# Moving the logs, powers and phases of two groups to other places in the instruction order of a fused GateLoop attention and gated layer

## The chip, the cores and the metric

The kernel runs on one core of a Trainium2 chip. The metric is the device time of one execution in microseconds. Several runs of a kernel are told by their median. A separate, profiled execution gives the trace from which the lines below come.

## The reference

```python
mag = np.sqrt(a_re * a_re + a_im * a_im)
scale = np.minimum(mag, 0.999) / (mag + 1e-06)
a_re_n, a_im_n = (a_re * scale, a_im * scale)
for t in range(S):
    ar, ai = (a_re_n[:, :, t, :, None], a_im_n[:, :, t, :, None])
    new_re = ar * S_re - ai * S_im
    new_im = ar * S_im + ai * S_re
    kv = np.einsum('bhd,bhe->bhde', k[:, :, t], v[:, :, t])
    S_re, S_im = (new_re + kv, new_im)
    y[:, :, t] = np.einsum('bhd,bhde->bhe', q[:, :, t], S_re)
x = y.transpose(0, 2, 1, 3).reshape(3072, 384)
h = x @ w_in                     # w_in 384 x 2048
out = (h * np.cos(h)) @ w_out    # w_out 2048 x 384
```

There are 4 batches, 8 heads, 768 steps and a head size of 48. The activations are 32-bit floats. The two weight matrices arrive as 64-bit floats.

## The kernel before

**Tiling.** The 3072 rows are cut into 24 chunks of 128 steps. Two chunks make a group, so there are twelve groups, numbered from 0. This text calls group 0 the first, group 1 the second and group 2 the third. Within a chunk the recurrence is turned into a masked product of keys and queries that carry cumulative decay and phase. A state of 96 x 48 a head passes from chunk to chunk.

**Steps of a group.** `log_steps` (line 731) squares `re` and `im` on ScalarE, and computes from them the log of the decay (`lg`) and the tangent of the half angle (`tan`), on ScalarE and VectorE in turn. Its last operation, the check, reads `re` once more and sums what is below zero; for group 0 it writes to `below`, for the others over `re` itself. `p_powers` (line 790) sums the logs along the steps on TensorE (`lgs`) and takes two exponentials (`P`, `Q`). `g_angle` (line 836) is the arctangent. `g_phase` (line 855) sums the angles on TensorE (`phs`), a chunk at a time, and subtracts the whole turns: a cast on ScalarE, then a subtraction on VectorE. For the second chunk of group 1 the sum takes in the reduced phase of the first. `p_even`, `p_apply`, `g_trig` and `g_stack` make from these the keys `ks` and the queries `qs`, 128 x 16 x 96 each. For groups 0 and 1 TensorE turns them (`f_turn`, `tp`), and ScalarE copies them to `kT` and `qT`. From group 2 on `f_transpose` (line 894) does it: VectorE transposes blocks of 32 x 32 (`tr`), and SP's queue writes them to DRAM (`moved`) and reads them back in order as `kT` and `qT`.

**Attention and layer.** `f_scores` multiplies keys and queries (`sc`) and masks them on VectorE (`atm`). `f_state` (`sp`) carries the state, `f_out` (`yp`) gives the rows, and `f_xt` (line 1003) takes them through DRAM (`x`, `xT`). `mm1` (line 1015) makes one of the eight tiles of h for a group (`hp`, 128 x 512 in one PSUM bank, six products); then ScalarE takes its sine with a shift of a quarter turn (`gate`) and, as a bound check, its square (`junk`), and VectorE multiplies gate and h. The tiles go in turn to three banks: two with the tag `m`, one with the tag `acc`. A fourth tile so waits for the gate of the first. `mm2` (line 1034) multiplies the gates with `w_out` (`op`), 16 products for a chunk. This holds for groups 0 and 1; later groups use a scheme with seven smaller products (`seventh`).

**Weights.** `weight` (line 596) fetches 1/8 of a matrix at a time as raw 64-bit words through GpSimd's queue into four buffers (`raw`). Each part takes a step on ScalarE and three on VectorE (`as_floats`, line 621). `into` lists the eight parts of `w_in`, `back` those of `w_out`. The first four of `w_in` are fetched at the start.

**Order.** Each engine runs its instructions in one order, which the build fixes. The activations that need a table (`special`) and all matrix products are chained in program order. The other operations go where the build's scheduler puts them. Between lines 1227 and 1255 the order of VectorE and ScalarE is written out by hand (`Ordered.by_hand`). After that `weave` (line 1140) merges lists of steps: each list gets a stretch between 0 and 1, and its steps are spread evenly in it. ScalarE's table for logs and exponentials is not the one for sine and arctangent; a change of table is a load (`ACT_TABLE_LOAD`). `load` (line 550) puts loads on SP's queue, and `logs(g)` (line 1176) ends with the load of the next group's `re` and `im`.

Of the kernel before, what the change touches and what calls it, by code (L numbers as in the profile page):

```python
# [11 lines left out]
F32 = mybir.dt.float32  # L12
# [475 lines left out]
def fast_path(ctx, tc, q, k, v, a_re, a_im, moe_w_in, moe_w_out, out, least, odd, wide):  # L488
# [9 lines left out]
    C = 128  # L498
    NCH = S // C
    G = 2  # L500
# [19 lines left out]
    stage = {"pool": room.enter_context(tc.tile_pool(name="stage", bufs=1)), "bufs": 4}  # L520
# [22 lines left out]
    X = [dict() for _ in range(NG)]  # L543
# [6 lines left out]
    def load(g, names, i=None, put=nc.sync.dma_start):  # L550
        for name in names:
            ap = {"re": a_re, "im": a_im, "q": q, "k": k, "v": v}[name]
            if name not in X[g]:
                X[g][name] = ld.tile([C, G, H, D], F32, tag=name, name=name,
                                     bufs=2 if name == "v" else 1)
            b, c = divmod(g * G + (i or 0), NCH)
            one, n = i or 0, G if i is None else 1
            steps = ap[b].rearrange("h (c p) d -> p c h d", p=C)[:, ds(c, n)]
            tile_ = X[g][name][:, ds(one, n)]
            parts = [(0, C, 0)]  # L560
            if name in ("re", "im") and g >= PEG:
# [10 lines left out]
        for i in range(G):  # L572
            load(0, names, i)
    ident = constant(np.eye(C, dtype=np.float32), "ident", pool=stage["pool"])
    sums = [constant(sums_np[0], "sums", pool=stage["pool"])]
    turns = [constant(sums_np[0] * np.float32(1.0 / math.pi), "turns", pool=stage["pool"])]
    last = constant(last_np, "last", pool=stage["pool"])
    carry = constant(carry_np, "carry")
# [200 lines left out]
    def summed_up(ps, g, i, name, ones):  # L779

        if g < PEG:
            matmul(ps, lhsT=ones, rhs=cut(X[g][name], i, 1), start=True, stop=True)
            return
        chunks_ = range(i + 1) if name == "tan" else [i]
        terms = [(half, c) for half in ("hi", "lo") for c in chunks_]
        for half, c in terms:
            matmul(ps, lhsT=exact if c == i else alls, rhs=cut(X[g][half], c, 1),
                   start=((half, c) == terms[0]), stop=((half, c) == terms[-1]))

    def p_powers(g, i):  # L790

        x = X[g]
        if i == 0:
            x["P"], x["Q"] = x["lg"], temp("Q")
            x["row"] = rows_d.tile([G * DM], F32, tag="row", name="row")
            x["end"] = ft.tile([D2, G * H], F32, tag="end", name="end")
        ps = pa.tile([C, DM], F32, tag="a", name="lgs")
        summed_up(ps, g, i, "lg", sums[0])
        special(out=cut(x["P"], i, 1), in_=ps, func=AF.Exp)
        special(out=cut(x["Q"], i, 1), in_=ps, func=AF.Exp, scale=-1.0)  # L800

# [34 lines left out]
    def g_angle(g, i, n):  # L836

        at = cut(X[g]["tan"], i, n)
        special(out=at, in_=at, func=AF.Arctan)
# [15 lines left out]
    def g_phase(g, i):  # L855

        x, n = X[g], g * G + i
        ps = pa.tile([C, DM], F32, tag="a", name="phs")
        early = g < PEG and n % NCH
        if not early:  # L860
            summed_up(ps, g, i, "tan", turns[0])
        else:
            matmul(ps, lhsT=turns[0], rhs=cut(x["tan"], i, 1), start=True, stop=False)
            matmul(ps, lhsT=last, rhs=before(n), start=False, stop=True)
        ph = cut(x["tan"], i, 1)
        scalar.copy(out=ph.bitcast(I32), in_=ps)
        vector.tensor_tensor(out=ph, in0=ps, in1=ph.bitcast(I32), op=ALU.subtract)
# [144 lines left out]
            out=xt.rearrange("p c g t -> p c (g t)"),  # L1012
            in_=moved.rearrange("p s d t -> (p s d) t").rearrange("(c r) t -> r c t", r=C))

    def mm1(g, jp):
        x = X[g]
        third = len(x.setdefault("gate", {})) % 3 == 2
        ps = pm.tile([C, 2, G * C], F32, tag="acc" if third else "m", name="hp",
                     bufs=1 if third else 2)
        for ji in range(2):  # L1020
            for dc in range(ND):
                matmul(ps[:, ji], lhsT=w_in[:, jp, dc, ts(ji, C)],
                       rhs=x["xT"][:, dc].rearrange("p g t -> p (g t)"),
                       start=(dc == 0), stop=(dc == ND - 1))
        gate = msb.tile([C, 2, G * C], F32, tag="gate", name="gate", bufs=8)
        junk = msb.tile([C, 2, G * C], BF16, tag="junk", name="junk", bufs=1)
        special(out=gate, in_=ps, func=AF.Sin, scale=1.0 / in_scale, bias=half_pi_b)
        scalar.activation(out=junk, in_=ps, func=AF.Square, scale=1.0 / in_scale,
                          accum_out=wide[:, ds(g * (NJ // 2) + jp, 1)])
        gated = vector.tensor_tensor(out=gate, in0=ps, in1=gate, op=ALU.mult)  # L1030
        x.setdefault("gated", gated)
        x["gate"][jp] = gate

    def mm2(g, i, j0, nj):
        if j0 == 0:
# [128 lines left out]
    def turned(g, i, name):  # L1164
        return [lambda hh=hh: f_turn(g, i, name, hh) for hh in range(2)]

    def prods(g):
        if not 0 <= g < NG:
            return
        for i in range(G):  # L1170
            yield lambda i=i: p_powers(g, i)
        yield lambda: g_angle(g, 0, G)
        yield lambda: g_carry(g)
        yield lambda: (p_even(g, 0, G), p_apply(g, 0, G))

# [63 lines left out]
    for i in range(2):  # L1239
        p_even(0, i, 1)  # L1240
    g_phase(0, 0)
    g_phase(0, 1)
    g_trig(0, 0, 1)
    p_apply(0, 0, 1)
# [6 lines left out]
    for t in (turned(0, 0, "kT") + turned(0, 0, "qT") + early[:1]  # L1251
              + [lambda: f_scores(0, 0), lambda: f_scores(0, 1)] + early[1:2]
              + turned(0, 1, "kT") + turned(0, 1, "qT") + early[2:3]
              + [lambda: p_end(0, 0, 2), lambda: f_state(0), lambda: f_rows(0)]
              + [lambda: f_scores(1, 0), lambda: f_scores(1, 1), lambda: f_columns(0)]
              + [lambda: f_state(1), lambda: busy(4), lambda: f_rows(1)] + early[3:4]
              + [lambda: busy(2), lambda: f_columns(1), lambda: busy(2)]
              + [lambda: next(one, None), lambda: next(two, None),
                             lambda: load(2, ("v",))]):
        t()  # L1260
    weave((logs(1), 0.0, 0.1), (convert(into[RAW:]), 0.0, 0.5),
          (first(0), 0.2, 1.0), (prods(1), 0.55, 0.58), ([lambda: load(2, ("k", "q"))], 0.58, 0.6),
          (phases(1), 0.7, 0.8), (keys(1), 0.8, 0.9), (convert(back[:4]), 0.5, 1.0))
    over = [t for i in range(G) for name in ("kT", "qT") for t in turned(1, i, name)]
    weave((convert(back[4:]), 0.0, 0.3), (second(0, 0), 0.0, 0.65), (over, 0.2, 0.6),
          (logs(2), 0.3, 0.31), (chunks(1), 0.7, 1.0), (prods(2), 0.85, 0.87))
    room.close()
    stage.update(pool=ctx.enter_context(tc.tile_pool(name="late", bufs=1)), bufs=1)
    weave((second(0, 1), 0.0, 0.35), (phases(2), 0.2, 0.3), (keys(2), 0.3, 0.45),
          (first(1), 0.4, 1.0))  # L1270
    for n in range(2, NG):
        weave((mixes(n - 1, 2, 4), 0.0, 0.12), (logs(n + 1), 0.0, 0.02), (chunks(n), 0.0, 0.36),
              (second(n - 1, 0), 0.0, 0.38), (products(n - 1, 0, 3), 0.0, 0.36),
# [82 lines left out]
```

## Time and profile before

| what | value |
|---|---|
| median of 3 runs | 675.01 us (674.88 to 675.69) |
| profiled execution | 674.87 us |
| its span | 673.0 us |
| mean granted TensorE clock | 0.986 |
| TensorE busy | 649.9 us |
| VectorE busy | 490.5 us |
| ScalarE busy | 396.5 us |
| ACT_TABLE_LOAD | 26 times, 33.4 us |
| first product of `hp` | at 45.08 us |
| first score of the second group | at 95.29 us |
| last product of `phs` of the third group | ends at 115.2 us |
| first score of the third group | at 139.07 us |

Times in the trace are microseconds from the start of the span. A row of a timeline gives start, length, engine, line, operation, what is written and what is read, a count, and in brackets how long the engine was idle before, and who released it. Many rows name the lines of helpers: 686 is every matrix product, 675 every VectorE or ScalarE operation that needs no table, 706 every activation that needs one. The tile's name tells the steps apart. [...] a product can stand as two records.

### The profile page before, as it was taken

How to read it: one execution, taken by the hardware profiler on the slowest of the kernel's cores; microseconds unless marked ns; L12 is line 12 of the kernel's file. 1: busy time of each engine (PE TensorE's matmuls, PEld its weight loads, DVE VectorE, ACT ScalarE, POOL GpSimd, SP SyncE). 2: the span in 40 equal slices, each digit the busy share in tenths (PEclk: the TensorE clock that was granted, in tenths of full speed). 3: DMA queues.
4: the chain of work that ended last, by engine and by line, in shares of the span. 5: the costliest groups of instructions: out<-in, count | busy, mean ns of one | idle time of the engine just before them, and what ended most of it. 6: DMA issues, size and time to landing. Idle time of an engine off the chain costs nothing.

```text
span 673.0 us, 10725 instructions
## 1 busy us (share of the span) xinstructions
PE 649.9 (97%) x4055; PEld 579.6 (86%) x4055; DVE 490.5 (73%) x793; ACT 396.5 (59%) x730; POOL 27.8 (4%) x47
## 2 busy tenths in 40 slices
PE   7897899999999999999999999999999999999995
PEld 5685677886899889999899999999999999999895
DVE  4989987668867867877768778868778768862241
ACT  6779875483574575476477467467467467332330
POOL 2012000000000000000000000000000000000000
PEclk8989989999999999999999999999999999999998
DMA  9788725814824845955945864864864862363000
GB/s 252 162 244 234 188 67 116 215 41 87 220 58 92 214 119 122 230 119 118 234 119 118 216 136 117 214 138 116 218 141 116 215 140 87 115 143 105 24 6 24
DMA packets 232810, 94.90 MB, mean 141 GB/s; under 512 B 208798, under 2 KB 221217, under 8 KB 232748
## 3 DMA queue, kind: packets, MB, share of 16 engines
q1 hardware_dynamic: 226252, 68.62, 45.2%
q0 software_dynamic: 5632, 25.17, 11.4%
q8 instruction: 34, 0.56, 0.3%
q10 hardware_dynamic: 864, 0.33, 0.2%
q14 instruction: 28, 0.23, 0.1%
HBM read 69.28 MB, written 24.81 MB: 140 GB/s over the span
## 4 chain that ended last, share of the span: by engine, by line
PE 80%; ACT 6%; DVE 6%; DMA 6%; issue 2%; SPq 0%; ACTq 0%; DVEq 0%
PE hp L686 32%; PE op L686 17%; PE sum L686 14%; PE yp L686 6%; PE sc L686 5%; PE sp L686 3%; PE phs L686 2%; DMA re<-in_a_re_dram 1%; PE lgs L686 1%; ACT raw L675 1%; DMA qT<-moved 1%; DMA raw<-in_moe_w_in_dram 1%; DVE mag L675 1%; DMA raw<-in_moe_w_out_dram 1%; DVE tan L675 1%
## 5 line engine op out<-in xcount | busy, mean ns | idle before, releaser
L686 PE MATMUL hp<-xT,w_in 128*128 128x256 f32 x1152 | 253.1, 381 | 1.3 <-DVE gate L675 0.9
L686 PEld LDWEIGHTS hp<-xT,w_in 128*128 128x128 f32 x1152 | 219.9, 191 | 33.3 <-DVE gate L675 1.8
L706 ACT ACTIVATE gate<-hp,half_pi_b 128x512 f32<-128x512 f32 x96 | 65.9, 687 | 127.6 <-PE hp L686 127.6
L686 PE MATMUL op<-w_out,gate 128*128 128x192 f32 (+1 forms) x448 | 103.7, 377 | 3.1 <-DVE w_out L675 3.1
L675 DVE TENSOR_TENSOR gate<-hp,gate 128x512 f32<-128x512 f32 x96 | 65.7, 685 | 55.8 <-ACT junk L675 55.8
L686 PEld LDWEIGHTS op<-w_out,gate 128*128 128x128 f32 x448 | 75.9, 191 | 19.7 <-DVE w_out L675 4.1
L675 ACT ACTIVATE junk<-hp 128x512 bf16<-128x512 f32 x96 | 56.5, 589 | 0.0
L686 PE MATMUL sum<-t_s,s 128*128 128x192 f32 x320 | 55.4, 327 | 0.0
L686 PEld LDWEIGHTS sum<-t_s,s 128*128 128x128 f32 x320 | 52.5, 191 | 0.3 <-DVE ot L675 0.3
L675 DVE TENSOR_TENSOR atm<-sc,causal 128x512 f32<-128x512 f32 x48 | 32.8, 687 | 24.8 <-PE sc L686 24.8
L686 PE MATMUL sc<-qT,kT 96*128 96x128 f32 x384 | 49.3, 276 | 1.4 <-ACT qT L675 0.8
L686 PEld LDWEIGHTS sc<-qT,kT 96*128 96x128 f32 x384 | 47.8, 192 | 3.2 <-ACT qT L675 1.1
L675 ACT ACTIVATE ot<-sum 128x192 f32<-128x192 f32 x30 | 9.5, 319 | 49.8 <-PE sum L686 49.8
L702 ACT ACT_TABLE_LOAD x26 | 33.4, 1283 | 4.0 <-DMA ident<-ident_const 3.6
L675 DVE SCALAR_TENSOR_TENSOR ot<-op,ot 128x192 f32<-128x192 f32 x31 | 11.0, 355 | 32.5 <-ACT ot L675 23.9
L675 ACT CAST tan<-phs 128x384 int32<-128x384 f32 x24 | 11.5, 478 | 39.2 <-PE phs L686 39.2
L686 PE MATMUL yp<-atm,v 128*48 128x128 f32 x352 | 33.6, 277 | 0.0
L686 PEld LDWEIGHTS sp<-v,ks 128*96 128x96 f32 x320 | 29.7, 165 | 0.0
L686 PE MATMUL yp<-qT,state 96*48 96x128 f32 x304 | 29.7, 272 | 0.0
L686 PE MATMUL sp<-v,ks 128*96 128x48 f32 x320 | 29.6, 246 | 0.0
L686 PE MATMUL sum<-w_out,gate 128*128 128x192 f32 x160 | 29.6, 329 | 0.0
L686 PE MATMUL op<-t_a,gate 128*128 128x192 f32 x160 | 29.0, 333 | 0.0
(138 smaller groups left out, 997.2 us busy)
## 6 DMA issues: line engine op xcount, KB each, us to landing
moved<-tr SPq DMA_DIRECT2D x20, 768.0 KB
raw<-in_moe_w_in_dram POOLq DMA_DIRECT2D x16, 768.0 KB, 5.8
raw<-in_moe_w_out_dram POOLq DMA_DIRECT2D x16, 768.0 KB, 4.7
kT<-moved SPq DMA_DIRECT2D x40, 192.0 KB
qT<-moved SPq DMA_DIRECT2D x10, 768.0 KB
k<-in_k_dram SPq DMA_DIRECT2D x24, 192.0 KB
q<-in_q_dram SPq DMA_DIRECT2D x24, 192.0 KB
v<-in_v_dram SPq DMA_DIRECT2D x24, 192.0 KB
```

The costliest lines, as they stand in the source:

```text
L675: ins = getattr(self.engine, op)(**kw)
L686: chain(nc.tensor.matmul(out, **kw), "tensor")
L702: chain(nc.scalar.preload_act_table_set(table))
L706: chain(nc.scalar.activation(func=func, **kw))
```

## The change

The rest of the diff renames `sums` to `upto`.

```diff
-    def mm1(g, jp):
-        x = X[g]
-        third = len(x.setdefault("gate", {})) % 3 == 2
-        ps = pm.tile([C, 2, G * C], F32, tag="acc" if third else "m", name="hp",
-                     bufs=1 if third else 2)
+    def mm1_sums(g, jp):
+        x = X[g]
+        x.setdefault("gate", {})
+        order = x.setdefault("order", [])
+        home = "mmcamcmm"[jp] if g == 0 else "mmc"[len(order) % 3]
+        order.append(jp)
+        pool, tag, bufs = {"m": (pm, "m", 2), "c": (pm, "acc", 1), "a": (pa, "a", None)}[home]
+        ps = pool.tile([C, 2, G * C], F32, tag=tag, name="hp", **({"bufs": bufs} if bufs else {}))
...
+        x.setdefault("hp", {})[jp] = ps
+
+    def mm1_gate(g, jp):
+        x = X[g]
+        ps = x["hp"].pop(jp)
...
+    def mm1(g, jp):
+        mm1_sums(g, jp)
+        mm1_gate(g, jp)
...
+    def powers(g):
+        return [lambda i=i: p_powers(g, i) for i in range(G)]
+
     def prods(g):
         if not 0 <= g < NG:
             return
-        for i in range(G):
-            yield lambda i=i: p_powers(g, i)
-        yield lambda: g_angle(g, 0, G)
+        if g not in (1, 2):
+            yield from powers(g)
+            yield lambda: g_angle(g, 0, G)
         yield lambda: g_carry(g)
         yield lambda: (p_even(g, 0, G), p_apply(g, 0, G))
...
     g_phase(0, 0)
+    next(one, None), next(two, None)
     g_phase(0, 1)
...
-              + [lambda: next(one, None), lambda: next(two, None),
-                             lambda: load(2, ("v",))]):
+              + [lambda: load(2, ("v",))]):
         t()
-    weave((logs(1), 0.0, 0.1), (convert(into[RAW:]), 0.0, 0.5),
-          (first(0), 0.2, 1.0), (prods(1), 0.55, 0.58), ([lambda: load(2, ("k", "q"))], 0.58, 0.6),
-          (phases(1), 0.7, 0.8), (keys(1), 0.8, 0.9), (convert(back[:4]), 0.5, 1.0))
+    later = convert(into[RAW:])
+    for t in (list(logs(1)) + later[:1] + sums(0, 0, 3) + powers(1) + later[1:2] + sums(0, 3, 4)
+              + [lambda: g_angle(1, 0, G)] + gates(0, 0, 2) + phases(1) + gates(0, 2, 4)
+              + later[2:]):
+        t()
+    weave((first(0)[4:], 0.0, 1.0), (prods(1), 0.1, 0.2),
+          ([lambda: load(2, ("k", "q"))], 0.3, 0.32),
+          (keys(1), 0.35, 0.5), (convert(back[:2]), 0.7, 1.0))
     over = [t for i in range(G) for name in ("kT", "qT") for t in turned(1, i, name)]
-    weave((convert(back[4:]), 0.0, 0.3), (second(0, 0), 0.0, 0.65), (over, 0.2, 0.6),
-          (logs(2), 0.3, 0.31), (chunks(1), 0.7, 1.0), (prods(2), 0.85, 0.87))
+    weave((convert(back[2:]), 0.0, 0.4), (second(0, 0), 0.05, 0.65), (over, 0.1, 0.6),
+          (chunks(1), 0.7, 1.0))
     room.close()
     stage.update(pool=ctx.enter_context(tc.tile_pool(name="late", bufs=1)), bufs=1)
-    weave((second(0, 1), 0.0, 0.35), (phases(2), 0.2, 0.3), (keys(2), 0.3, 0.45),
-          (first(1), 0.4, 1.0))
+    for t in (list(logs(2)) + second(0, 1) + sums(1, 0, 2) + powers(2) + sums(1, 2, 3)
+              + [lambda: g_angle(2, 0, G)] + gates(1, 0, 3)):
+        t()
+    weave((first(1)[3:], 0.0, 1.0), (prods(2), 0.0, 0.02), (phases(2), 0.1, 0.3),
+          (keys(2), 0.35, 0.6))
```

`mm1` is split: `mm1_sums` is its products, `mm1_gate` its gate, square and multiplication. `sums` and `gates` list these for a range of tiles. The fourth `hp` tile of group 0 takes a bank of the pool `pa`, which the attention uses.

No operation is added or dropped but loads of ScalarE's table: the path that runs has 24 in place of 26. What moves on TensorE's queue, as the two builds have it (products of a kind in brackets):

```
before, group 1: hp(24) lgs hp(6) phs hp(6) phs hp(12), then op(16) with tp among them, scores
after,  group 1: hp(18) lgs hp(6) phs phs hp(24), then op(16) with tp among them, scores
before, group 2: scores of group 1 with lgs among them, op(12) phs op(4) hp(48), scores
after,  group 2: scores of group 1, op(16) hp(12) lgs hp(12) phs hp(24), scores
```

On ScalarE the check of group 0 stands between the casts of its two phases instead of behind copies of `kT` and `qT`; the powers of group 1 stand ahead of all gates of group 0; the powers and the arctangent of group 2 stand behind the last `ot` copy and ahead of the gates of group 1; the sines of group 2 stand behind the gate of the fifth `hp` tile. On VectorE the first part of `w_out` ends behind the last gate of group 0 and the keys of group 1; before, it ended ahead of the fifth gate. On SP's queue the load of `re` for group 1 stands ahead of four small loads of `end`, and the load of `v` for group 3 ahead of `xT` of group 1.

More of the change, by code (lines that the diff above doesn't have):

```diff
@@ L574, in fast_path @@
     ident = constant(np.eye(C, dtype=np.float32), "ident", pool=stage["pool"])
-    sums = [constant(sums_np[0], "sums", pool=stage["pool"])]
+    upto = [constant(sums_np[0], "sums", pool=stage["pool"])]
     turns = [constant(sums_np[0] * np.float32(1.0 / math.pi), "turns", pool=stage["pool"])]
@@ L797, in p_powers @@
         ps = pa.tile([C, DM], F32, tag="a", name="lgs")
-        summed_up(ps, g, i, "lg", sums[0])
+        summed_up(ps, g, i, "lg", upto[0])
         special(out=cut(x["P"], i, 1), in_=ps, func=AF.Exp)
@@ L1257, in fast_path, with sums, gates @@
               + [lambda: busy(2), lambda: f_columns(1), lambda: busy(2)]
-              + [lambda: next(one, None), lambda: next(two, None),
-                             lambda: load(2, ("v",))]):
-        t()
-    weave((logs(1), 0.0, 0.1), (convert(into[RAW:]), 0.0, 0.5),
-          (first(0), 0.2, 1.0), (prods(1), 0.55, 0.58), ([lambda: load(2, ("k", "q"))], 0.58, 0.6),
-          (phases(1), 0.7, 0.8), (keys(1), 0.8, 0.9), (convert(back[:4]), 0.5, 1.0))
+              + [lambda: load(2, ("v",))]):
+        t()
+    def sums(g, lo, hi):
+        return [lambda jp=jp: mm1_sums(g, jp) for jp in range(lo, hi)]
+    def gates(g, lo, hi):
+        return [lambda jp=jp: mm1_gate(g, jp) for jp in range(lo, hi)]
+    later = convert(into[RAW:])
[6 more added lines that the diff above has]
+          (keys(1), 0.35, 0.5), (convert(back[:2]), 0.7, 1.0))
     over = [t for i in range(G) for name in ("kT", "qT") for t in turned(1, i, name)]
-    weave((convert(back[4:]), 0.0, 0.3), (second(0, 0), 0.0, 0.65), (over, 0.2, 0.6),
-          (logs(2), 0.3, 0.31), (chunks(1), 0.7, 1.0), (prods(2), 0.85, 0.87))
+    weave((convert(back[2:]), 0.0, 0.4), (second(0, 0), 0.05, 0.65), (over, 0.1, 0.6),
+          (chunks(1), 0.7, 1.0))
     room.close()
     stage.update(pool=ctx.enter_context(tc.tile_pool(name="late", bufs=1)), bufs=1)
-    weave((second(0, 1), 0.0, 0.35), (phases(2), 0.2, 0.3), (keys(2), 0.3, 0.45),
-          (first(1), 0.4, 1.0))
+    for t in (list(logs(2)) + second(0, 1) + sums(1, 0, 2) + powers(2) + sums(1, 2, 3)
[3 more added lines that the diff above has]
+          (keys(2), 0.35, 0.6))
     for n in range(2, NG):
```

## The prediction

> **What bounds the kernel now.** I read the page's busy shares first, then TensorE's waits, then the stages, then the hand-over into the third group. The span is 673.0 us and the execution took 674.87 us, 0.14 us below the median of 675.01.
>
> ```profile
> PE 649.9 (97%) x4055; PEld 579.6 (86%) x4055; DVE 490.5 (73%) x793; ACT 396.5 (59%) x730; POOL 27.8 (4%) x47
> ```
>
> TensorE bounds it: 23.1 us idle in all. From the timeline, 6.9 us of that lie before 28 us and 7.2 us in the last stretch, from 600 us on; neither is touched. TensorE's waits (total, times, longest) name what is left:
>
> ```profile
> PE op L686 <- DVE w_out L675: 3.1, 1, 3.1
> PE phs L686 <- ACT tan L706: 3.1, 2, 2.9
> ...
> PE hp L686 <- DVE gate L675: 0.9, 2, 0.7
> ```
>
> Three of these, 0.73 + 2.88 + 3.14 = 6.75 us, lie between 54 and 84 us. That is what the change can take away. The stages show who sets that region (after the colon: length, busy PE, PEld, DVE, ACT, POOL, granted clock, DMA):
>
> ```profile
> 54.00:58.00 4.00, 3.27 (x15) 2.78 (x15) 4.00 (x8) 4.00 (x9) 0.52 (x1) 1.00 1.12 317
> 58.00:64.00 6.00, 3.50 (x15) 2.48 (x13) 6.00 (x9) 5.94 (x11) 1.44 (x2) 1.00 0.86 224
> 64.00:68.00 4.00, 3.62 (x8) 2.27 (x9) 4.00 (x6) 2.99 (x7) 0.72 (x1) 0.57 0.61 184
> ...
> 80.00:84.00 4.00, 0.86 (x4) 0.20 (x2) 4.00 (x9) 3.08 (x5) 0.00 (x0) 1.00 0.43 173
> ```
>
> VectorE is full in each, so moving its work about frees nothing by itself; and the clock is 0.57 just after a wait of 2.9 us. Then TensorE's timeline (start, length) around the third group:
>
> ```profile
> 115.00 0.34 PE L686 MATMUL phs<-lo,exact 128*128 128x384 f32 x1
> 115.18 2.74 PE L686 MATMUL op<-w_out,gate 128*128 128x384 f32 x8
> 117.76 8.04 PE L686 MATMUL hp<-xT,w_in 128*128 128x256 f32 x36
> 126.01 13.22 PE L686 MATMUL hp<-xT,w_in 128*128 128x256 f32 x60 [0.22 <-DVE gate L675]
> 139.07 1.06 PE L686 MATMUL sc<-qT,kT 96*128 96x128 f32 x8
> ```
>
> Between the last phase product and the first score lie 23.9 us of TensorE work. Under it runs the way from phases to turned queries. On SP's queue:
>
> ```profile
> 123.19 2.54 SPq L906 DMA_DIRECT2D moved<-tr  x2
> 127.14 3.89 SPq L909 DMA_DIRECT2D kT<-moved  x4
> 131.14 1.06 SPq L911 DMA_DIRECT2D qT<-moved  x1
> ```
>
> The stage 132 to 136 us has a DMA share of 1.00, 136 to 140 one of 0.10: qT lands near 136.4, 2.7 us ahead of its use. So cast, sines, products, two transposes and transfers take 136.4 - 115.2 = 21.2 us, all but 2.7 of 23.9 us.
>
> **What the Trainium skill says.** "TensorE: Matmul & The Clock Gate", What's actually happening: an idle TensorE falls to half clock and recovers after about 3.4 us of work. The trace agrees: the first phase product after the 2.88 us wait took 1.44 us, warm ones 0.65; together with what follows the two long waits cost 1.5 and 1.7 us more. The same page, Part 2: What happens when you issue a matmul, keeps matmuls in program order; "Perfetto Trace Analysis", Tensor Engine Instruction (MATMUL, LD_WEIGHTS), calls ScalarE and VectorE strict queues: a late operand stops all behind it. The trace agrees: the second group's logarithm, its input ready by 42.1 us, stood until 44.84 behind copies of which the first waited for TensorE until 43.03. "ScalarE: Activation LUTs", What ACT_TABLE_LOAD costs: 1283 ns and a drain of about 1380; here 1.28 us and the next operation starts at once (59.24 to 60.53), so I price 1.28.
>
> **The change, part by part.** Starts below that are not in the trace are my estimates, walked along the built queues with the trace's durations: VectorE start to start 0.87 us at 768 wide, 0.47 at 384 or for a one-input operation, 0.60 for a gate; on ScalarE a gate and its square 1.15, a weight part 0.9, four powers 1.5.
>
> *First check.* Its two operations (0.5 us each) move from 29.9 and 32.3 us into a ScalarE gap of 1.59 us (19.69 to 21.28): free. The second group's `re`, whose buffer they release, goes out near 24.3 us rather than 33.0, on SP's queue now ahead of four tiny `end` loads that VectorE needs at 36.3. The squares come near 30 us, not 39.5. Yet the logarithm stands on ScalarE behind the xT copy (44.47) in both queues: 44.84 as before. The squares stand ahead of four copies that TensorE needs at 34.5 and that ended at 32.4: room for 1.8 us if `re` is late. Value 0; bounds a gain of 0.6, a loss of 0.8.
>
> *Second group.* Two table loads (2.6 us of ScalarE) go away, and the 0.73 us wait. hp tiles 0 to 2 fill three banks until 54.0, sums of logs to 55.3, hp 3 to 58.0 in a bank of the other pool. ScalarE, done with logs at 51.4, idles until 54.8 for the sums, then powers 56.3, table 57.6, arctangent 58.4: the phase product waits 0.45 instead of 2.88. But the second half's phase needs the reduced first one, whose cast stands behind two gates (58.4 + 2.3 = 60.7, plus subtraction, behind a gate and a conversion step: 62.2); TensorE waits 1.8. hp 4 to 7 then run 62.9 to 73.3. VectorE after 62.2: gates 2 and 3 (64.0), even powers and phase (67.1), bit mask and k product (68.4), gate 4 behind three weight parts on ScalarE (69.2), then q product, gates 5 to 7 and the four key products (76.9). Only there does the first w_out part end, near 77.8; before, at 65.8. TensorE waits for it from 73.3, and for the second part to 81.4. At 2.2 us a part, plus two steps of the next logs (1.8), the eighth is done near 95.0; before, 93.3. The last two products take 1.3: the second group's scores start at 96.3 instead of 95.3. So VectorE takes back what the waits gave. Value +1.0; bounds -1 (if VectorE loses its extra second of waiting for gates) and +3.
>
> *Third group, to its phases.* Attention takes 10.3 us (11.0 less the 0.7 us of log sums that leave it): 106.6. Sixteen op products, 10.2: 116.8, against twelve before. hp 0 and 1: 122.0. Log sums 0.7, hp 2: 125.3. hp 3 needs the bank of hp 0, and its gate now stands behind powers (123.8), table and arctangent (125.9): gate 127.05, product 127.7. Wait 2.5 (bounds 1.5 and 3.5). It ends at 130.4; the split of the angles, behind two more gates, is done at 131.0; phases end 132.2. Half a chance of a cold clock after that wait adds 0.6: 132.8. Before: 115.2. Difference 17.6 us. The v load of the fourth group goes past xT on SP's queue; xT, some 115 to 117 us, is needed at 116.8: value 0, at most 1.5.
>
> *Third group, from its phases on.* The sines stand behind gate 4, which waits for hp 4: phases + 2.6 + 1.2, then 0.8: the first key product starts 4.6 us after the phases instead of 2.2, and gate 5 takes 0.6 of VectorE ahead of the transposes. So the way grows from 21.2 to 24.2 us. The cover is now four hp tiles, 10.4 us. TensorE waits 13.8 us; scores start near 157.0, before 139.07: +17.9. This includes all above. Without the extra gates the wait is 10.8; with the slower way of the fourth group (tr at 224.0, landing 242.3, 18.3 instead of 15.5) it is 16.6.
>
> *After it.* A cold clock after such a wait: +1.6 (0.5 to 2). Later stages keep their order and were TensorE-bound, with waits of half a microsecond; nothing there can give back more than one.
>
> Sum: 674.87 + 17.9 + 1.6 = 694.4; the median lies 0.14 above: 694.5.
>
> **The rivals.** *All waits vanish*: 675.0 less 6.75 and less some 3 of cold clock gives 665. For it: two fewer table loads, an earlier `re`. It decides at the end of hp 7: qT would have to land 10.4 us after the phases, in half of its measured 21.2. Against it: VectorE is full. Chance 0.06; this is the faster side. *Only the way of the keys counts*: the first part breaks even, hp 3 hardly waits, no gate delays the sines: phases at 126 or so, wait 10.8, cold 1.6, about 687.5. Chance 0.22. *VectorE falls further behind*: the w_out parts come after keys and gates, and each gap on VectorE for a gate is lost; +4 more, slow way of the keys, about 700. Chance 0.14. *The parts cancel* within 0.2%: 675, chance 0.02. That the change does not do what it says is excluded: the built queues show each move.
>
> **How the numbers follow.** The forecast has 0.56, with 690 to 698 of its own. The range 687 to 701 takes in both slower rivals; the outer bounds of single terms would have to coincide to leave it. About 0.2% is what a measurement here can tell from no change. Faster 0.06, same 0.02, slower 0.92.
>
> **What would show it.** 24 table loads instead of 26. TensorE waiting for w_out from about 73 us for more than 4 us, in place of 3.1. hp of the second group waiting for a gate by 2 to 3 us near 125. Above all, sc waiting for qT (DMA) by 11 to 17 us near 142 to 157, and a lower clock just after. I am wrong if that last wait is below 5 us: then the way of the keys is shorter than the 21.2 us it took, or the phases do not come after half of the hp tiles.

## The result and the profile after

The changed kernel takes 699.66 us (median of 4 runs, 699.21 to 700.97), the kernel before on the same chip 675.35 us (674.88 to 676.34): a ratio of 1.0361, 95% interval 1.0342 to 1.0380. The forecast was 694.5 with a range up to 701. The profiled span grew from 673.0 to 697.7 us, so 24.7 us are to be found. First the engines' busy time in the profile after:

```profile
PE 654.5 (94%) x4055; PEld 581.6 (83%) x4055; DVE 490.8 (70%) x793; ACT 392.6 (56%) x728; POOL 28.1 (4%) x47
```

TensorE is busy 4.6 us longer with the same 4055 records of products, so those ran slower. The other 20.1 us of the span are idle time. Its waits (total, times, longest) in the profile after:

```profile
PE sc L686 <- DMA qT<-moved: 16.4, 2, 15.1
...
PE op L686 <- DVE w_out L675: 5.2, 3, 4.4
...
PE hp L686 <- DVE gate L675: 3.2, 1, 3.2
...
PE phs L686 <- DVE tan L675: 2.1, 2, 1.6
PE phs L686 <- ACT tan L706: 1.4, 2, 0.8
```

The wait of the phases for the arctangent fell from 3.1 to 1.4 us. Each of the others grew, or is new. One alone is 15.1 us. The timeline of TensorE in the profile after shows where it stands:

```profile
124.28 2.75 PE L686 MATMUL hp<-xT,w_in 128*128 128x256 f32 x12
130.22 4.54 PE L686 MATMUL hp<-xT,w_in 128*128 128x256 f32 x12 [3.19 <-DVE gate L675]
...
135.47 0.34 PE L686 MATMUL phs<-lo,exact 128*128 128x384 f32 x1
135.65 10.52 PE L686 MATMUL hp<-xT,w_in 128*128 128x256 f32 x48
161.31 2.05 PE L686 MATMUL sc<-qT,kT 96*128 96x128 f32 x8 [15.15 <-DMA qT<-moved]
163.15 3.81 PE L686 MATMUL op<-w_out,gate 128*128 128x384 f32 x8
```

The fourth `hp` tile of the second group waits 3.19 us for the gate that frees its bank, and then takes 4.54 us where the one before took 2.75. The third group's phases end at 135.65 (before: 115.18). From there to the first score only four tiles, 10.52 us, lie on TensorE. SP's queue in the profile after tells what the score waits for:

```profile
146.87 2.54 SPq L906 DMA_DIRECT2D moved<-tr  x2
150.19 4.11 SPq L909 DMA_DIRECT2D kT<-moved  x4
154.40 1.20 SPq L911 DMA_DIRECT2D qT<-moved  x1
```

The first write goes out 11.2 us after the phases' end, behind the last `hp` product (146.2). So no work of TensorE covers the transfers. The stages in the profile after (columns as in the prediction):

```profile
54.00:58.00 4.00, 3.65 (x16) 2.59 (x14) 4.00 (x6) 3.52 (x6) 0.93 (x1) 1.00 1.11 296
58.00:64.00 6.00, 4.10 (x14) 2.56 (x15) 5.24 (x9) 6.00 (x16) 1.44 (x2) 1.00 1.08 294
64.00:68.00 4.00, 4.00 (x20) 3.54 (x19) 4.00 (x6) 4.00 (x7) 0.00 (x0) 1.00 0.36 151
...
146.00:161.00 15.00, 0.17 (x1) 0.00 (x0) 11.12 (x13) 10.48 (x15) 0.00 (x0) 0.57 0.94 228
161.00:165.00 4.00, 3.69 (x11) 2.88 (x12) 0.69 (x1) 0.00 (x0) 0.00 (x0) 0.50 0.73 129
```

From 54 to 68 us TensorE does more than before (11.75 us busy instead of 10.39), and VectorE is no longer quite full in one stage. Yet the gain is gone at the first `w_out` part. From 146 to 161 us TensorE stands and the DMA engines work at a share of 0.94. In the next 4 us the granted clock is 0.50. Below, a clock of 0.50 is called low.

### The profile page after: what moved, and what is told of

Its sections match the earlier page's. It is cut to its first block, busy times and chain, and to the rows that moved or that the text cites. A ratio compares the mean times of both kernels' runs of the same rounds, so it can differ in the third digit from the quotient of the medians.

```text
span 697.7 us, 10727 instructions
## 1 busy us (share of the span) xinstructions
PE 654.5 (94%) x4055; PEld 581.6 (83%) x4055; DVE 490.8 (70%) x793; ACT 392.6 (56%) x728; POOL 28.1 (4%) x47
## 4 chain that ended last, share of the span: by engine, by line
PE 80%; ACT 6%; DVE 6%; DMA 5%; issue 1%; SPq 1%; ACTq 0%; DVEq 0%
PE hp L686 32%; PE op L686 16%; PE sum L686 14%; PE yp L686 5%; PE sc L686 5%; PE sp L686 3%; DMA qT<-moved 2%; PE phs L686 2%; DVE mag L675 1%; PE lgs L686 1%; ACT raw L675 1%; DMA raw<-in_moe_w_in_dram 1%; PE yr L686 1%; DVE w_out L675 1%; PE tp L921 1%
## 5 line engine op out<-in xcount | busy, mean ns | idle before, releaser
L686 PE MATMUL op<-w_out,gate 128*128 128x192 f32 (+1 forms) x448 | 107.0, 385 | 5.2 <-DVE w_out L675 5.2
L686 PEld LDWEIGHTS op<-w_out,gate 128*128 128x128 f32 x448 | 77.5, 194 | 24.3 <-issue 9.1
L675 ACT COPY yT<-yp 48x512 f32<-48x512 f32 x44 | 25.2, 573 | 20.0 <-PE yp L686 19.5
```

The costliest lines, as they stand in the source:

```text
L675: ins = getattr(self.engine, op)(**kw)
L686: chain(nc.tensor.matmul(out, **kw), "tensor")
```

## The experiments

Each kernel is the kernel before or the changed kernel with the edit shown. A ratio is to runs of the kernel before on the same chip (medians 675.19 to 675.88 in the four groups of runs).

### The first check alone

```diff
 (kernel before)
     g_phase(0, 0)
+    next(one, None), next(two, None)
     g_phase(0, 1)
...
-              + [lambda: next(one, None), lambda: next(two, None),
-                             lambda: load(2, ("v",))]):
+              + [lambda: load(2, ("v",))]):
```

> The kernel before with the first check moved between the two phases, and nothing else. Main theory (the loss is made at the third group): the two operations fit ScalarE's gap near 20 us, so 675.0 to 676.0; the first hp product started 0.67 us later in the trace after, so up to +0.7 may be the check's. Rival (the earlier re load and the squares ahead of the copies disturb the first group): 676 or more, with the first hp product at 45.7 us or later.

Measured: 675.74 us, ratio 1.0007 (0.9996 to 1.0017). The first `hp` product starts at 45.15 us, before at 45.08. This part costs and gains nothing that these runs can tell.

### The second group's part alone

```diff
 (changed kernel; all of the third group as before)
-        if g not in (1, 2):
+        if g != 1:
...
-          (chunks(1), 0.7, 1.0))
+          (logs(2), 0.3, 0.31), (chunks(1), 0.7, 1.0), (prods(2), 0.85, 0.87))
...
-    for t in (list(logs(2)) + second(0, 1) + sums(1, 0, 2) + powers(2) + ...
+    weave((second(0, 1), 0.0, 0.35), (phases(2), 0.2, 0.3), (keys(2), 0.3, 0.45),
+          (first(1), 0.4, 1.0))
```

> The changed kernel with the third group's part undone (logs, powers, phases and keys of the third group where they were before). Main theory: sc no longer waits for qT; what stays is the second group's part, whose scores began 1.8 us late: 676.5 to 677.5. Rival (VectorE's late w_out parts are passed on and carry most of the loss): 685 or more.

Measured: 680.23 us, ratio 1.0078 (1.0056 to 1.0101). Both numbers were missed: alone, this part costs 4.9 us. TensorE waits for `w_out` five times, 8.7 us in all, and the second group's scores start at 99.67 us. VectorE's and TensorE's timelines there show two of the reasons:

```profile
93.37 0.95 DVE L675 SCALAR_TENSOR_TENSOR mag<-re,mag 128x768 f32<-128x768 f32 x1
94.24 0.55 DVE L675 TENSOR_SCALAR lg<-lg 128x768 f32<-128x768 f32 x1
...
95.58 0.95 DVE L675 TENSOR_TENSOR lg<-lg,rs 128x768 f32<-128x768 f32 x1
96.44 0.95 DVE L675 CUSTOM_DVE_ANT_0 w_out<-raw,w_out 128x1536 uint16<-128x1536 uint16 x1
...
97.45 2.43 PE L686 MATMUL op<-w_out,gate 128*128 128x384 f32 x4 [2.13 <-DVE w_out L675]
99.67 2.78 PE L686 MATMUL sc<-qT,kT 96*128 96x128 f32 x16
```

The last step of the last `w_out` part runs at 96.44, in the changed kernel at 94.72. Four log steps of the third group stand between the parts here, two in the changed kernel; the two more (0.47 and 0.87 us from start to start) make 1.3 of these 1.7 us. The second reason is the clock. Behind the wait of 2.13 us it is low from 98.0 to 101.4 us, which at half speed costs 1.7 us; in the changed kernel it is 1.00 there.

A third cause, raw words that come late, scatters. VectorE stood for them near 83 us for 0.54 us here and 0.67 us in the changed kernel. Six kernels of this study have the second group's order of the change. In their profiles the second group's scores start at 97.06, 97.13, 97.85, 98.98, 99.67 and 99.72. In two of them VectorE stood near 92 to 94 us for a raw part, 1.32 and 1.77 us. Five kernels with the old order and the old logs of the second group gave 95.06, 95.25, 95.29, 95.92 and 97.45. The means are 98.4 and 95.8. So this part delays the scores by some 2.6 us, and single profiles differ by 2 us and more. How the 4.9 us divide between log steps, late transfers and clock in the runs that were not profiled, stays open.

### The second group's logs in idle time

Here the log steps are put into the first group's attention, in the old order otherwise.

```diff
 (kernel before, with the first check moved)
+    ahead = log_steps(1, 0, G)
...
+              + [lambda: next(ahead)]
               + [lambda: f_scores(1, 0), lambda: f_scores(1, 1), lambda: f_columns(0)]
-              + [lambda: f_state(1), lambda: busy(4), lambda: f_rows(1)] + early[3:4]
+              + [lambda: next(ahead)]
+              + [lambda: f_state(1), lambda: busy(4), lambda: next(ahead), lambda: f_rows(1)]
+              + early[3:4] + [lambda: next(ahead)]
...
-    weave((logs(1), 0.0, 0.1), (convert(into[RAW:]), 0.0, 0.5),
+    weave(([lambda: list(ahead), lambda: load(2, ("re", "im"))], 0.0, 0.1), ...
```

> The kernel before with the check moved, and with the second group's log steps placed so that the logarithm and the exponentials stand ahead of the last copies on ScalarE, in its idle stretch from 38.9 to 43.0 us; nothing else moved. If VectorE's idle 2.7 us at 44.7 and ScalarE's unbroken queue from 43 to 69 us are what holds the second group's phases: the waits of TensorE for the arctangent (2.9) and for w_out (3.0) shrink to less than half and the time falls by 3 to 6, 669 to 672. Rival (VectorE's total work up to 93 us is the bound whatever the order, or the copies in front of the first hp product come late): 674 to 677.

Measured: 675.11 us, ratio 0.9988 (0.9979 to 0.9996). The rival held. ScalarE was done with the logs at 46.6 us instead of 51.4, as meant. ScalarE's timeline in this kernel shows why that gained little:

```profile
57.64 0.68 ACT L706 ACTIVATE gate<-hp,half_pi_b 128x512 f32<-128x512 f32 x1
...
58.92 1.28 ACT L702 ACT_TABLE_LOAD   x1
60.21 0.49 ACT L706 ACTIVATE lg<-lgs 128x384 f32<-128x384 f32 x1
...
63.16 0.84 ACT L706 ACTIVATE tan<-tan 128x768 f32<-128x768 f32 x1
```

The powers stand behind four gates, so the arctangent runs at 63.16 as it did before, and TensorE waits 3.6 us for it. The wait for `w_out` is 3.2 us. Logs that are ready sooner do not help while their reader's place is fixed. These 0.8 us are the only gain over the kernel before in this study, and the profile does not show where they come from: the third group's scores start at 140.20 us there, before at 139.07.

### The third group's part alone

```diff
 (kernel before; mm1 split as in the change)
-        for i in range(G):
-            yield lambda i=i: p_powers(g, i)
-        yield lambda: g_angle(g, 0, G)
+        if g != 2:
+            yield from powers(g)
+            yield lambda: g_angle(g, 0, G)
...
-          (logs(2), 0.3, 0.31), (chunks(1), 0.7, 1.0), (prods(2), 0.85, 0.87))
+          (chunks(1), 0.7, 1.0))
...
-    weave((second(0, 1), 0.0, 0.35), (phases(2), 0.2, 0.3), (keys(2), 0.3, 0.45),
-          (first(1), 0.4, 1.0))
+    (the third group's part of the change)
```

> The kernel before with the third group's part alone (second group's powers, hp tiles and check as before). Main theory: nearly the whole loss, 697 to 699, with sc waiting some 15 us for qT. Rival (the early part carries the loss): below 686.

Measured: 699.02 us, ratio 1.0332 (1.0305 to 1.0358). TensorE's waits in this kernel:

```profile
PE sc L686 <- DMA qT<-moved: 15.9, 2, 15.2
PE hp L686 <- DVE gate L675: 4.9, 2, 3.2
```

Both waits of the changed kernel are there, and all but 0.6 us of its time, which is less than the runs differ (695.23 to 700.05). So the parts don't add: 4.9 alone and 23.7 alone give 24.3 together.

### The third group turned on TensorE

To see what the wait for `qT` is worth, this kernel does without VectorE's transposes and the transfers. TensorE turns the third group's keys and queries, as it does for the first two: 32 more products, no write to and read from DRAM.

```diff
 (changed kernel)
-        if g < PEG:                       (queries)
+        if g <= PEG:
...
-                if g >= PEG:              (keys)
+                if g > PEG:
...
+    ident = ft.tile([C, C], F32, tag="tr", name="ident_again")
...
+    for t in [t for i in range(G) for name in ("kT", "qT") for t in turned(2, i, name)]:
+        t()
```

> The changed kernel, but the third group's keys and queries are turned by TensorE, as those of the first two groups are, instead of by VectorE's transposes and DRAM; 32 more products, some 3.5 us. Main theory (TensorE waits 15 us for the transfers of the turned queries, and runs at a cold clock after it): the scores start near 150 us instead of 161, no wait for qT there, 685 to 688. Rival (the wait is only where the late phases show; sines and gates on ScalarE would hold the scores as long): 694 or more.

Measured: 685.68 us, ratio 1.0133 (1.0113 to 1.0152), as the theory had it. TensorE's timeline in this kernel:

```profile
136.92 10.52 PE L686 MATMUL hp<-xT,w_in 128*128 128x256 f32 x48
147.28 1.04 PE L921 MATMUL tp<-ident_again,ks 128*96 128x128 f32 x8
...
150.77 1.11 PE L686 MATMUL sc<-qT,kT 96*128 96x128 f32 x8
```

The scores follow the turns with no wait. They start at 150.77 instead of 161.31, though 3.5 us of turns were added and the phases came 1.3 us later. So the way over VectorE's transposes and DRAM is shown as the cost, taken as one. Left over the kernel before are 9.8 us. The second group's part, the late phases and the turns stay in; they were not measured apart.

### The clock kept up during the wait

Here TensorE multiplies blocks of `w_in` into an unused tile while it would wait. Nobody reads the tile.

```diff
 (changed kernel)
+    ps = pa.tile([C, 512], F32, tag="a", name="fill")
+    for _ in range(16):
+        matmul(ps, lhsT=w_in[:, 0, 0, 0:C], rhs=w_in[:, 0, 0:2].rearrange("p a b -> p (a b)"),
+               start=True, stop=True)
```

> The changed kernel with 16 products of 512 columns, results unused, ahead of the third group's scores: they fill some 14 us of the wait for qT. Main theory (2 us after the wait are the cold clock): the clock just after stays 1.0 and the time falls by 1.5 to 2.5, 697.2 to 698.2. Rival (the slow products after the wait have another cause, such as the mask or operands that come late): 699.2 to 700.2, no change.

Measured: 697.55 us, ratio 1.0316 (1.0297 to 1.0334), 2.1 us less than the changed kernel (2.6 when each is taken against the kernel before on its own chip). TensorE's timeline in this kernel:

```profile
146.17 13.90 PE L686 MATMUL fill<-w_in 128*128 128x512 f32 x32
162.12 1.13 PE L686 MATMUL sc<-qT,kT 96*128 96x128 f32 x8 [2.06 <-DMA im<-in_a_im_dram]
```

Each of the 16 products stands as two records. The scores still start near 162 (the view puts the rest of the wait down to a load of `im`; they read `kT` and `qT`). But the first eight records take 1.13 us where they took 2.05, and the granted clock from 160 to 164 us is 1.00. So about 2 us of the loss are the low clock after the wait. The profile after gives the same: the clock there stays low until 165.3, 4.0 us behind the first score, and at half speed this costs 2.0 us. "TensorE: Matmul & The Clock Gate" of the Trainium skill, What's actually happening, has an idle TensorE fall to half clock after an idle window of about 3.4 us, and come back after about 3.4 us of work. The 0.50 over the 4 us after the wait and 0.97 over the next 5 us agree with the return. On the fall the measurement decides: waits of 1.96 and 2.13 us, shorter than that window, were followed by a low clock in three kernels of this study.

### The phases back ahead of the hp tiles

The kernels from here on keep the third group's logs and powers behind the attention, and put its phases ahead of all `hp` tiles again.

```diff
 (changed kernel)
-    for t in (list(logs(2)) + second(0, 1) + sums(1, 0, 2) + powers(2) + sums(1, 2, 3)
-              + [lambda: g_angle(2, 0, G)] + gates(1, 0, 3)):
+    for t in (list(logs(2)) + second(0, 1)[:1] + powers(2) + [lambda: g_angle(2, 0, G)]
+              + second(0, 1)[1:3] + list(prods(2)) + phases(2) + second(0, 1)[3:]):
         t()
-    weave((first(1)[3:], 0.0, 1.0), (prods(2), 0.0, 0.02), (phases(2), 0.1, 0.3),
-          (keys(2), 0.35, 0.6))
+    weave((keys(2), 0.0, 0.2), (first(1), 0.1, 1.0))
```

> The changed kernel, but the third group's powers and phases stand between the op products instead of behind four hp tiles; its logs stay behind the attention. Main theory (it is the place of the phases against hp that counts, not that of the logs): sc waits less than 1 us for qT, 677 to 679. Rival (late logs, or loads on SP's queue that collide with the transfers, cost by themselves): 688 or more.

Measured: 686.31 us, ratio 1.0157 (1.0138 to 1.0176). The wait for `qT` is gone, as the theory said, but its time was missed by 8 us. A new wait took the place. ScalarE's timeline in this kernel:

```profile
128.56 0.84 ACT L706 ACTIVATE lg<-tan 128x768 f32<-128x768 f32 x1 [4.70 <-DMA row<-lg]
```

The sine writes over the buffer `lg`, from which a small transfer still has to read a row. That transfer stands on SP's queue behind the loads of `k`, `q` and `im`:

```profile
122.66 1.01 SPq L567 DMA_DIRECT2D k<-in_k_dram  x2
123.77 1.50 SPq L567 DMA_DIRECT2D q<-in_q_dram  x2
125.32 0.92 SPq L567 DMA_DIRECT2D im<-in_a_im_dram  x1
126.34 0.26 SPq L818 DMA_DIRECT2D row<-lg  x1
```

SP's queue had itself stood until 122.66, 6.6 us for VectorE, which still read the buffer of `k`. The gates stand behind the sine on ScalarE, and so TensorE's fourth `hp` tile waits 4.8 us. The next kernel takes that wait away by moving the loads:

```diff
 (the kernel just above)
-          (chunks(1), 0.7, 1.0))
+          (list(chunks(1))[:-1], 0.7, 1.0))
...
-    weave((keys(2), 0.0, 0.2), (first(1), 0.1, 1.0))
+    weave((keys(2), 0.0, 0.2), (first(1), 0.1, 1.0), (list(chunks(1))[-1:], 0.3, 0.31))
```

> The kernel with the third group's phases ahead of all hp tiles, but the loads of k, q and v for the fourth group are put behind the write of the decay row on SP's queue. In the run before, the sines waited 4.7 us for that write (row, which reads the buffer that the sine overwrites), and an hp tile 4.8 us for its gate behind them. If that is what kept it 9 us from the kernel before: 679 to 682, sc waiting under 1 us for qT. Rival (the late logs and powers cost by themselves): stays at 685 to 687.

Measured: 680.02 us, ratio 1.0058 (1.0037 to 1.0079), as expected: the sine starts at 121.34 with no wait, and TensorE shows the third group's scores at 142.78 (`issue` names no releaser):

```profile
142.78 1.13 PE L686 MATMUL sc<-qT,kT 96*128 96x128 f32 x8 [0.68 <-issue]
```

So of the change's 24.3 us, some 20 (24.3 less the 4.1 that are left) hang on where the phases stand, with the powers and the arctangent ahead of them, provided the row goes ahead of the loads.

### What is left of the third group's part

The kernel just above, with the second group in the old order:

```diff
 (kernel before)
-        for i in range(G):
-            yield lambda i=i: p_powers(g, i)
-        yield lambda: g_angle(g, 0, G)
+        if g != 2:
+            yield from powers(g)
+            yield lambda: g_angle(g, 0, G)
...
-          (logs(2), 0.3, 0.31), (chunks(1), 0.7, 1.0), (prods(2), 0.85, 0.87))
+          (list(chunks(1))[:-1], 0.7, 1.0))
...
-    weave((second(0, 1), 0.0, 0.35), (phases(2), 0.2, 0.3), (keys(2), 0.3, 0.45),
-          (first(1), 0.4, 1.0))
+    (third group as just above)
```

> The kernel before with the third group's part of the last trial alone: its logs, powers and phases behind the second group's attention, the phases still ahead of every hp tile, the row's write ahead of the loads. The second group's order is that of before. Main theory: the eighth part of w_out loses the two log steps that stood in front of it on VectorE, so the second group's scores start near 93 us instead of 95.3; the stretch from those scores to the third group's takes about 45.7 us as in the last trial, against 43.8 before. The sum is nought: 675 to 677, that is 3 to 5 below the last trial (680.0), which is then what the second group's own reordering cost there. Rival: the log steps moved out come back in full on the way to the phases, and the second group's reordering cost nothing: 679 to 681.

Measured: 680.07 us, ratio 1.0068 (1.0047 to 1.0090). The rival's number came, but not its reason, and the theory's premise failed too. The log steps did not leave the stretch of the `w_out` parts (one still runs at 91.23 us): VectorE's order is left to the build's scheduler, and a later place in the list doesn't bind it. What moved are the powers, which are chained. The arctangent runs at 111.54 instead of 104.89. VectorE's timelines, first before and then here, show what follows:

```profile
115.19 1.25 DVE L675 TENSOR_TENSOR tan<-phs,tan 128x384 f32<-128x384 f32 x2 [2.89 <-ACT tan L675]
...
115.69 0.95 DVE L675 SCALAR_TENSOR_TENSOR Q<-mag,Q 128x768 f32<-128x768 f32 x1
116.56 0.55 DVE L675 TENSOR_TENSOR tan<-phs,tan 128x384 f32<-128x384 f32 x1
117.03 0.95 DVE L675 TENSOR_TENSOR Q<-k,Q 128x768 f32<-128x768 f32 x1
117.89 0.95 DVE L675 TENSOR_TENSOR mag<-q,lg 128x768 f32<-128x768 f32 x1
118.76 0.55 DVE L675 TENSOR_TENSOR tan<-phs,tan 128x384 f32<-128x384 f32 x1
```

Before, the even powers and their products were done by 112.3, under the `op` products, and both subtractions ran from 115.19, one right behind the other. Now they stand among the subtractions, and the second one starts at 118.76. So the sine starts at 119.34 instead of 116.48, and the first write goes out at 126.61 instead of 123.19. TensorE then waits for the scores:

```profile
142.48 2.05 PE L686 MATMUL sc<-qT,kT 96*128 96x128 f32 x8 [2.38 <-issue]
```

They start at 142.48 instead of 139.07, and the clock is low from 142.4 to 145.8, which costs another 1.7 us. Together this is 5.1 us, near the measured 4.9. The later write alone does not give this wait, since before `qT` landed an estimated 2.7 us ahead of its use. From the first write to the score it took 15.9 us here, 14.7 in the kernel above, 13.2 before (to the estimated landing). Here the loads of `k`, `q` and `v` stand directly ahead of the writes on SP's queue; whether they hold up the transfers was not tried apart. The second group's order made no difference to the time here: 680.02 us with it, 680.07 without. Without it the second group's scores start at 95.06 instead of 97.06, but the third group's come alike (142.48 and 142.78).

The next kernel adds the edit of "The second group's logs in idle time" to this one:

> The same, on top of the trial with the second group's log steps spread into the idle time of the first group's attention. Main theory: the second group's logs leave VectorE's full stretch as well, but its sum of work up to the last part of w_out is nearly the same, so no more than 1 us is gained: 674 to 676. Rival: with both sets of log steps gone VectorE is no longer full between 54 and 84 us, and the waits for w_out and the arctangent go: 670 to 673.

Measured: 679.73 us, ratio 1.0071 (1.0058 to 1.0084); both expectations fell with the premise above. The third group's scores start at 141.97, after a wait of 1.69 us, and the clock is low from 143.2 to 146.6.

Last, the sines ahead of the output copy on ScalarE and both transposes ahead of the gates on VectorE:

```diff
 (third group's part alone, as above; in mm2 the copy is chained behind the sines)
-              + second(0, 1)[1:3] + list(prods(2)) + phases(2) + second(0, 1)[3:]):
+              + second(0, 1)[1:3] + list(prods(2)) + phases(2) + list(keys(2)) + second(0, 1)[3:]):
...
-    weave((keys(2), 0.0, 0.2), (first(1), 0.1, 1.0), (list(chunks(1))[-1:], 0.3, 0.31))
+    weave((first(1), 0.0, 1.0), (list(chunks(1))[-1:], 0.3, 0.31))
...
+            if (g, i) == (0, 1):
+                chain(copied, "scalar")
```

> The trial of the third group's part alone, with its sines ahead of the output copy (ot) of the first group's last op part on ScalarE, and no gate between its two transposes on VectorE. Main theory: what that trial lost (the third group's scores at 142.5 us instead of 139.1) is the sine, which stood 2.1 us for the product before the copy, and the gate of 0.6 us between the transposes; with both gone the writes start near 124 us, qT lands ahead of the last hp product, and only the 0.8 us by which the phases are later is left: scores at 139.8 to 140.5, 675.5 to 677. Rival: the loads of k, q and v, which now stand directly ahead of the writes on SP's queue, keep the transfers where they were: scores at 142 or later, 679 to 681.

Measured: 679.43 us, ratio 1.0059 (1.0043 to 1.0075). The theory fell. The timelines of ScalarE and TensorE in this kernel (the profiled execution took 682.14 us, the longest of the six):

```profile
121.73 0.84 ACT L706 ACTIVATE lg<-tan 128x768 f32<-128x768 f32 x1 [2.73 <-DVE tan L675]
...
131.23 14.90 PE L686 MATMUL hp<-xT,w_in 128*128 128x256 f32 x60 [1.96 <-DVE gate L675]
145.97 1.06 PE L686 MATMUL sc<-qT,kT 96*128 96x128 f32 x8
```

The sine waits for VectorE's subtraction, not for the copy. And TensorE now waits 1.96 us for a gate that stands behind both transposes, at a clock of 0.59 from 132 to 136 us. The rival's numbers came (679.43, scores at 145.97), but not its reason: the scores follow the last `hp` product with no wait for `qT`. With the early logs of the second group on top:

> The same on top of the trial with the second group's log steps spread into the first group's attention: all moves of the change in the places that cost least. Main theory: the second group's scores gain at most 0.5 us and the third group's follow them: 674.5 to 676. Rival: with the third group's way of keys hidden again, the earlier second group counts in full: 672 to 674.

Measured: 680.34 us, ratio 1.0072 (1.0055 to 1.0089); both missed. No kernel with the third group's powers behind the second group's attention came below 679 us.

## Why the prediction was right, and where its sizes were off

The sign and the mechanism held: the wait of `sc` for `qT` in one piece, the lower clock behind it, the waits for `w_out` and for a gate, and 24 table loads. The size was too small: the forecast was 19.5 us over the kernel before, the measured loss is 24.3. So 699.66 lies above the 690 to 698 that the forecast gave its own mechanism. It lies inside the range since that takes in a slower rival near 700, whose main reason hardly came; that much was luck. The steps in order:

**First check**: nought, as forecast. In the profile after the first `hp` product starts 0.67 us later than before, but with the check moved alone 0.07; the 14 profiles lie between 44.95 and 46.00.

**Second group**: the wait for the arctangent was 0.65 us (forecast 0.45), that for the reduced first phase 1.60 (1.8), the first `w_out` part ended at 77.6 (77.8), its wait was 4.38 (4.5), the last part ended at 95.7 (95.0). The scores start at 97.13 instead of 96.3: +1.84 for +1.0, inside its bounds. The order on VectorE is the forecast one:

```profile
73.58 0.95 DVE L675 TENSOR_TENSOR qs<-mag,lg 128x768 f32<-128x768 f32 x1
...
76.67 0.94 DVE L675 CUSTOM_DVE_ANT_0 w_out<-raw,w_out 128x1536 uint16<-128x1536 uint16 x1
```

What the sum left out is that late conversions free the raw buffers late. GpSimd stood 15.91 us for VectorE, the last four parts were fetched between 78 and 88 us, and VectorE stood 0.67 us for one of them, in other profiles up to 1.77. Alone, this part went beyond the upper bound of +3.

**Third group, to its phases**: forecast +17.6, measured +20.5. Of these 2.9 us, 0.8 came from the second group. Attention took 10.85 us (forecast 10.3). The bank wait was 3.19 (2.5): the gate came at 129.48, behind the carried phase and an even power on VectorE. The tile after it took 1.4 us more than one at full clock, where the forecast gave a cold (low) clock half a chance and 0.6. The prediction's own evidence had both its waits of some 3 us cost more (1.5 and 1.7). Of 20 such waits in the 14 profiles 15 were followed by a low clock (see the last section), so half a chance was too little, and the full cost would not have been sure either.

**From the phases on**: forecast 24.2 us, measured 25.66 to the first score. That the sines stand behind the fifth gate held (ScalarE, profile after):

```profile
138.44 0.69 ACT L706 ACTIVATE gate<-hp,half_pi_b 128x512 f32<-128x512 f32 x1 [1.62 <-PE hp L686]
...
139.59 0.84 ACT L706 ACTIVATE lg<-tan 128x768 f32<-128x768 f32 x1
```

The first key product starts 4.8 us after the phases (forecast 4.6). Most of the rest is in the transfers: 14.4 us from the first write's issue to the score, where before it was 13.2 to the estimated landing. Loads of `re` go out right behind them, at 156.21, and may share the DMA engines; that wasn't tried. The wait of 15.15 us lies in the forecast's 10.8 to 16.6.

**After it**: from the first score to the first state product it took 6.38 us, before 4.37: 2.0 instead of 1.6 us, and the filled wait bears it out with 2.1 to 2.6.

The scores' shift and this make 22.24 + 2.0 = 24.2 of the 24.7 us. So the mis-sized terms are the hand-over to the phases (+2.9) and the way behind them (+1.5), all on the slow side.

**The rivals.** The case in which VectorE falls further behind named 700. Its terms, 4 more from the `w_out` parts and 2.8 for the slower way of the keys, make 701.3; in the trace of the change they are 0.8 and 1.5. In the case of the keys alone, phases at 126 do not go with its 687.5: four `op` products (2.6) and four `hp` tiles (10.4) behind 115.2 make 128.2.

## What to carry to other kernels

A latency chain that runs through several engines and DRAM is hidden only by the work that stands behind its start and ahead of its end on the bounding engine; when its start is moved, count that cover first, since waits of 3 us elsewhere don't weigh against it. An operation moved later takes along whatever depends on it on other engines, and a small transfer that holds a buffer can become the longest wait if it falls behind large loads on its queue. After a wait of some 3 us on TensorE, allow for a low clock: 15 of 20 such waits brought one here, most of them for 3.4 us, which costs 1.7.

## What the runs showed of the hardware

- The low clock comes in steps. Read in windows of a quarter of a microsecond, it lasts 3.41 us or a whole multiple of that (6.8, 10.2, 17.1) in every one of the 14 profiles, and within a profile all low stretches begin on one grid of 3.41 us. In the profile after three of them begin at 76.55, 131.16 and 148.22: 16 steps and 5 steps apart.
- So not only the length of a wait counts, but where it falls on the grid. Of 20 waits of 2.8 to 3.8 us between 40 and 175 us, 15 were followed by a low clock, 11 for one step and 4 for two. The waits of 3.55 us ("The second group's logs in idle time") and 3.77 us (the last kernel) were not; the grid cuts them near the middle (at 62.5 of 60.5 to 64.1, at 62.4 of 60.5 to 64.2). In the last two kernels 1.96 us that lay between two steps of the grid were enough.
- One step under steady work costs half its length: the `hp` tile after the wait of 3.19 us took 4.04 us to the next product's start, one at full clock 2.6. Products into an unused tile over 13.9 of the 16 us of a wait kept the granted clock at 1.00, although 2.06 us of it stayed idle.
- The 3 KB row transfer held the sine for 4.70 us, since it stood on SP's queue behind loads of `k`, `q` and `im`. Its own issue took 0.26 us. Ahead of the loads the sine did not wait.
- The start of one and the same stage scatters between profiles. In the changed kernel, the third group turned on TensorE and the filled wait, VectorE and ScalarE run the same operations in the same order up to the second group's scores; these start at 97.13, 98.98 and 97.85 us.
